# Block 0 of a token mixer's input: from one transposing DMA and a partly loaded strip to four plain loads and transposes on TensorE

## The chip, the cores and the metric

The kernel runs on one core of a Trainium2 chip. The metric is the device time of one execution in microseconds (us). Lower is better. The profile is of one execution on that core.

## The reference

All tensors are bfloat16. S = 2048 tokens, D = 512, 32 heads of 16. A branch (attention over 8 keys at distances 0, 2, ..., 14) and B branch (an MLP over the tokens) read the same x and are mixed by a gate.

```python
x = A_x                                                   # 2048 x 512
g = sigmoid((x * gate_w).sum(-1, keepdims=True))
q, k, v = split(x @ A_wqkv)                               # heads of 16
logits[s, w] = (q[s] . k[s - 2w]) * 16**-0.5              # w = 0..7, masked before the start
a = (softmax(logits) applied to v[s - 2w]) @ A_wo
h = layernorm(x)
u = gelu(einsum("sd,sf->df", h, B_w1) + B_b1)             # f = 1792, contraction over tokens
b = einsum("df,fs->sd", u, B_w2) + B_b2
return g * a + (1 - g) * b
```

## The kernel before

The kernel keeps everything in one arena of on-chip memory and names views of it. `X` holds x with tokens on the partitions (16 tiles of 128 tokens). `XT` holds x transposed, the 512 columns as four blocks `dt` of 128 partitions by 2048 tokens. `WQKV`, `W1W`, `W2S` and `WO` are the weights, `Q5`, `K5`, `V5` the projections, and `ps` is the accumulator memory of eight banks of 512 floats per partition.

The stages are these. TensorE first projects: for a token block `sb` of 512 and a quarter `dl` of the head dimensions, four matmuls (one for each `dt`) sum into one bank (`f_proj`, L613 to L621), and ScalarE (ACT) copies the bank to `Q5`, `K5` or `V5` (`f_evq`, L626 and L629). VectorE (DVE) multiplies Q by shifted K (L689), and TensorE sums the products over a head (L697). Between and after these TensorE does the MLP's two products (L811 and L861), and at the end the output product (L877), whose result DVE mixes with the gate (L898) before it is stored. DVE also takes the row statistics of the layer norm (L573, which reads `X`), the softmax and the sums over the values.

The order on each engine comes from a list scheduler (`_Sched`). Each operation is added by `A(engine, function, duration, reads, writes, ...)`, and the names in `reads` and `writes` give its waits. `chain([...])` (L958 on) fixes by hand the order on DVE and ACT. Loads are issued with `sch.dma(queue, ...)` on SP or ACT; on SP each load comes after the one before it (`prev_dma`) and waits for the one five back (`throttle`), through the list `init_dmas`. The attribute `lands` gives the scheduler a landing time of the first loads, and their waits are cleared.

Token block 0 is projected before the others, in an order that follows the landing of its parts: `pf_*`, L633 to L640. All eight banks are used, four for Q (`acc0` to `acc3`) and four for K (`lg4` to `lg7`). The four Q banks take `dt` 0, then 1, 2 and 3; then the four K banks take `dt` 0 and 1, then 2 and 3: 32 matmuls of 512 columns.

What block 0 needs comes in this way. ACT loads columns 0 to 127 of the first four x tiles into `XP` (L479), and then Wq's first 128 rows. SP issues a transposing DMA of columns 128 to 511 into `XT` blocks 1 to 3 (`ld_xt0`, L473), then Wq's other three parts, Wk in two loads, x tiles 0 and 1 (`ld_x`, for L573), the transposing DMA of block 1 (`ld_xt(1)`, L460), and x tiles 2 and 3. TensorE runs warm-up matmuls on constants (L536), transposes the four tiles of `XP` by a matmul with an identity (`f_tr`, L544), and runs two more warm-up matmuls. ACT (L554) and DVE (L556) copy the halves of the result to `XT` block 0. Only then, and when Wq's first part has landed, the projections begin.

Of the kernel before, what the change touches and what calls it, by code (L numbers as in the profile page):

```python
# [5 lines left out]
BF16 = mybir.dt.bfloat16  # L6
# [3 lines left out]
AF = mybir.ActivationFunctionType  # L10
# [323 lines left out]
def bass_gated_mix__sliding_local_dilated__mixer_token_mlp__prompt_kernel(nc, A_x, A_wqkv, A_wo, B_x, B_w1, B_b1, B_w2, B_b2, gate_w, out, dbg=None):  # L334
    with contextlib.ExitStack() as es:
        view, pview, off, total = _views(nc, es)
        ps = es.enter_context(nc.psum_tensor("ps", [128, 8, 512], FP32))
        esem = {e: es.enter_context(nc.semaphore("sem_" + e)) for e in ("pool", "act", "dve", "pe")}
        sch = _Sched()

        x2d = A_x[0]
        xv = x2d.rearrange("(t p) d -> p t d", p=128)
# [5 lines left out]
        X = view("X", BF16, [(D, NST), (1, D)])  # L348
        XT = view("XT", BF16, [(S, 4), (1, S)])
# [19 lines left out]
        IDENT = view("IDENT", BF16, [(1, 128)])  # L369
# [45 lines left out]
        A = sch.add  # L415
# [12 lines left out]
        def mk_dma(dst, src):  # L428
            return lambda e: e.dma_start(dst, src)  # L429

        init_dmas = []
# [4 lines left out]
        def prev_dma():  # L436
            return [init_dmas[-1]] if init_dmas else []

        def ld_x(t0, n, q="sp"):
            ds = sch.dsem("x%d" % t0)  # L440
            op = sch.dma(q, mk_dma(X[:, t0:t0 + n, :], xv[:, t0:t0 + n, :]), n * 128 * D * 2, ds,
                         writes=["x%d" % t for t in range(t0, t0 + n)], deps=throttle() if q == "sp" else [], after=prev_dma() if q == "sp" else [], name="d_x%d" % t0)
            if q == "sp":
                init_dmas.append(op)
            return op

        def ld_w(tn, d0, n, q="sp"):
            ds = sch.dsem("wqkv%d_%d" % (tn, d0))
            op = sch.dma(q, mk_dma(WQKV[:, d0:d0 + n, tn * D:(tn + 1) * D], wqkv_v[:, d0:d0 + n, tn * D:(tn + 1) * D]),
                         n * 128 * D * 2, ds, writes=["wqkv%d_%d" % (tn, dt) for dt in range(d0, d0 + n)],  # L450
                         deps=throttle() if q == "sp" and n == 4 else [], after=prev_dma() if q == "sp" else [],
                         issue=0.65 if n == 4 else 0.45, name="d_wp%d_%d" % (tn, d0))
            if q == "sp":
                init_dmas.append(op)
            return op
# [5 lines left out]
                         writes=["xt_%d" % t for t in range(4 * sb, 4 * sb + 4)], deps=throttle(), after=prev_dma(), name="d_xt%d" % sb)  # L461
            init_dmas.append(op)

        XT0 = ["xt0_%d" % d for d in range(4)] + ["xt0_0b"]
        ALLXT = XT0 + ["xt_%d" % t for t in range(4, NST)]

        def xt_of(sb, d0=0, d1=4):
            return XT0[d0:d1] + (XT0[4:] if d0 == 0 else []) if sb == 0 else ["xt_%d" % t for t in range(4 * sb, 4 * sb + 4)]

        def ld_xt0():  # L470
            ds = sch.dsem("xt0")
            dst = XT[:, 1:4, 0:512]
            op = sch.dma("sp", lambda e: e.dma_start_transpose(dst, x2d[0:512, 128:512]), 512 * 384 * 2, ds, issue=1.25,  # L473
                         writes=XT0[1:4], after=prev_dma(), name="d_xt0")
            init_dmas.append(op)
            return op

        XP = view("OUTS", BF16, [(128, 4), (1, 128)])
        d_xp = sch.dma("act", mk_dma(XP, xv[:, 0:4, 0:128]), 512 * 128 * 2, sch.dsem("xp"), writes=["outs0"], issue=0.4, name="d_xp")  # L479

        first_loads = [ld_w(0, 0, 1, "act"), ld_xt0(), ld_w(0, 1, 1), ld_w(0, 2, 1), ld_w(0, 3, 1), ld_w(1, 0, 2), ld_w(1, 2, 2),
                       ld_x(0, 2)]
        ld_xt(1)
        first_loads.append(init_dmas[-1])
        for op_, t_ in zip(first_loads, (3.4, 4.6, 5.0, 5.4, 5.8, 6.6, 7.4, 8.2, 10.6)):
            op_.lands = t_
            op_.deps.clear()
        d_xp.lands = 3.1
        first_loads[0].order.add(d_xp)
        init_dmas[:] = [first_loads[1]] + first_loads[5:]  # L490
        ld_x(2, 2)
        ld_x(4, 4)
        ld_xt(2)
        ld_xt(3)
# [5 lines left out]
        def ld_w1(j):  # L500
# [4 lines left out]
            if j < 4:  # L505
# [8 lines left out]
                       writes=["wo"], deps=throttle(), after=prev_dma(), name="d_wo")  # L514
# [4 lines left out]
        for i_, (v_, n_) in enumerate(((B_b1, NFT), (B_b2, NST))):  # L519
            vr = v_.rearrange("(t q j) -> q t j", q=4, j=32)  # L520
            for q_ in range(4):
                sch.dma("sp", mk_dma(psub(BR, 32 * q_, n_, 32 * i_, [(1, 32)]), vr[q_]), n_ * 64, ds_b, reads=["br"],
                        writes=["br_%d_%d" % (i_, q_)], deps=throttle(), after=prev_dma(), name="d_b_%d_%d" % (i_, q_), issue=0.45)
        d_w1.append(ld_w1(3))
        A("dve", lambda e: e.transpose(out=BT, in_=BR), 0.2, reads=["br_%d_%d" % (i_, q_) for i_ in range(2) for q_ in range(4)],
          writes=["btc"], name="t_b")
# [3 lines left out]
        CONE = nc.const_aps.tensor(1.0, [128, D], BF16)  # L530

        def f_warm(n, w_=D):
            def fn(e):
                ins = None
                for _ in range(n):
                    ins = e.matmul(ps[:, 7, 0:w_], lhsT=CONE[:, 0:128], rhs=CONE[:, 0:w_], start=True, stop=True)  # L536
                return ins
            return fn

        def f_tr(h):  # L540
            def fn(e):
                ins = None
                for t in range(2):
                    ins = e.matmul(ps[:, 5 + h, 128 * t:128 * t + 128], lhsT=XP[:, 2 * h + t, :], rhs=IDENT, start=True, stop=True)  # L544
                return ins
            return fn

        A("pe", f_warm(5), 2.13, writes=["lg7_0", "lg7_1"], name="warm1", prio=-100)
        w2_ = A("pe", f_warm(1, 256), 0.2, writes=["lg7_0", "lg7_1"], name="warm2", prio=-100)
        ta_ = A("pe", f_tr(0), 0.215, reads=["outs0", "ident"], writes=["lg5_0", "lg5_1"], after=[w2_], name="tr0", prio=-100)  # L550
        tr_ = A("pe", f_tr(1), 0.215, reads=["outs0", "ident"], writes=["lg6_0", "lg6_1"], after=[ta_], name="tr1", prio=-100)
        A("pe", f_warm(1), 0.43, writes=["lg7_0", "lg7_1"], after=[tr_], name="warm3", prio=-100)
        w3_ = A("pe", f_warm(1, 256), 0.2, writes=["lg7_0", "lg7_1"], after=[tr_], name="warm4", prio=-100)
        A("act", lambda e: e.activation(out=XT[:, 0, 0:256], in_=ps[:, 5, 0:256], func=AF.Copy), 0.35, reads=["lg5_0", "lg5_1"],  # L554
          writes=["xt0_0"], name="ev_tra", prio=0)
        A("dve", lambda e: e.tensor_copy(out=XT[:, 0, 256:512], in_=ps[:, 6, 0:256]), 0.35, reads=["lg6_0", "lg6_1"],  # L556
          writes=["xt0_0b"], name="ev_trb", prio=0)

        JK = view("OUTS", BF16, [(1, D)], extra=0)
        def cols(v_, lo, n, step=1):  # L560
# [9 lines left out]
        for hf in range(2):  # L570
            t0 = 8 * hf
            for t in range(t0, t0 + 8):
                A("dve", (lambda t_: (lambda e: e.bn_stats(out=ST6[:, t_, :], in_=X[:, t_, :])))(t), 0.59,  # L573
                  reads=["x%d" % t], writes=["st6_%d" % t], name="ln1_%d" % t, prio=0)
# [13 lines left out]
              reads=["zc%d" % hf], writes=["sd%d" % hf], name="ln_sqrt%d" % hf, prio=0)  # L588
            A("dve", (lambda t0_: (lambda e: e.reciprocal(out=cols(RSTD, t0_, 8), in_=cols(SD, t0_, 8))))(t0), 0.25,
              reads=["sd%d" % hf], writes=["rstd%d" % hf], name="ln_rstd%d" % hf, prio=0)  # L590
            A("dve", (lambda t0_: (lambda e: e.scalar_tensor_tensor(
                out=cols(NMR, t0_, 8), in0=mv(t0_, 0), scalar=-0.5, in1=cols(RSTD, t0_, 8),
# [38 lines left out]
        tnames = ["q", "k", "v"]  # L631
        first = [(tn, dl) for tn in range(2) for dl in range(4)]
        fbn = [["acc%d" % b] for b in range(4)] + [["lg%d_0" % b, "lg%d_1" % b] for b in range(4, 8)]  # L633
        for (b0, d0, d1, s0, s1) in ((0, 0, 1, 0, 512), (0, 1, 2, 0, 512), (0, 2, 3, 0, 512), (0, 3, 4, 0, 512), (4, 0, 2, 0, 512), (4, 2, 4, 0, 512)):
            for b in range(b0, b0 + 4):
                tn, dl = first[b]
                last_main[0] = A("pe", f_proj(tn, dl, 0, b, d0, d1, s0, s1), 0.216 * (d1 - d0) * (s1 - s0) / 512,
                                 reads=xt_of(0, d0, d1) + ["wqkv%d_%d" % (tn, dt) for dt in range(d0, d1)],
                                 writes=fbn[b], after=[last_main[0]], name="pf_%s%d_%d_%d" % (tnames[tn], dl, d0, s0))
                last_main[0].order.add(w3_)  # L640
        for b, (tn, dl) in enumerate(first):
            A("act", f_evq(tn, dl, 0, b), 0.52, reads=fbn[b] + (["k5pad"] if tn == 1 else []),
              writes=["%s5_%d_0" % (tnames[tn], dl)], name="ev_%s%d_0" % (tnames[tn], dl), prio=0)
# [7 lines left out]
        for (tn, dl, sb) in seq_proj:  # L651
# [18 lines left out]
                writes=["xa"] + ["wqkv%d_%d" % (tn, dt) for tn in range(3) for dt in range(4)], name="d_xa")  # L670
# [271 lines left out]
        def chain(names):  # L942
            for a_, b_ in zip(names, names[1:]):
                byname[b_].order.add(byname[a_])

        def ln1(*ts):
            return ["ln1_%d" % t for t in ts]

        def ln2(hf):
            return ["ln2%s%d" % (c_, hf) for c_ in "abcd"]  # L950
# [4 lines left out]
        def lnr(hf):  # L955
            return ["ln_rstd%d" % hf, "ln_nmr%d" % hf]

        chain(["rp", "ev_trb"] + ln1(0, 1, 2, 3) + ["qkm_0_0_0", "qkm_0_1_0"] + ln1(4, 5, 6, 7) + ln2(0)  # L958
              + ["qkm_0_2_0"] + lnr(0) + ["qkm_0_3_0", "qkm_0_0_2"] + ln1(8, 9) + ["qkm_0_1_2", "qkm_0_2_2", "qkm_0_3_2"] + ln1(*range(10, 16)) + ln2(1)
              + ["t_b", "qkm_1_0_0"] + lnr(1) + ["qkm_1_1_0"]  # L960
              + ["qkm_1_2_0", "qkm_1_3_0"] + gz(12, 13, 14, 15) + ["msk_0", "sm_ma0", "sm_mb0"] + gz(0, 1, 2) + [
# [90 lines left out]
```

## Time and profile before

| what | us |
|---|---|
| median of three runs | 168.57 (167.89 to 170.0) |
| the profiled execution | 168.47 |
| its span (first to last instruction) | 167.1 |
| TensorE (PE) busy | 163.1 |
| weight loads (PEld), beside PE | 77.7 |
| VectorE (DVE) busy | 151.3 |
| ScalarE (ACT) busy | 75.1 |

Times in the views count from the start of the span. A name with a small q (SPq, ACTq) is an engine's instruction queue; a DMA row on it tells when the transfer was issued and for how long that held the queue, not when it landed. Matmuls are pipelined: their start-to-start distance is their cost, and the mean duration of one is longer. Loads that plain DMAs bring show as `DMA_DIRECT2D`, transposing ones as `DMA_TRANSPOSE`. The granted clock was 1.00 throughout.

### The profile page before, as it was taken

To read this page: it belongs to the slowest core of one execution; us is meant where nothing else is said; L and a number is where in the kernel's file an instruction comes from. 1 tells how busy PE (TensorE), PEld (TensorE's weight loads), DVE (VectorE), ACT (ScalarE), POOL (GpSimd) and SP (SyncE) were. 2 spreads that over 40 slices of the span, in tenths; PEclk is the share of its full clock that TensorE was granted. 3 is DMA by queue.
4 is the path that set the end of the run, shared out by engine and by line. 5 is a ranking of instruction groups with operands and counts; after the bars stand their busy time and mean duration, and the time that the engine had idled before them with its cause. 6 is when DMAs were issued, how large, how long until landed. Compare 5 with 4: busy or idle time off the path is not lost.

```text
span 167.1 us, 2152 instructions
## 1 busy us (share of the span) xinstructions
PE 163.1 (98%) x860; PEld 77.7 (47%) x860; DVE 151.3 (91%) x154; ACT 75.1 (45%) x116; POOL 0.7 (0%) x8
## 2 busy tenths in 40 slices
PE   7799999999999999999999999999999999999994
PEld 3355555554554444444444444444444444444463
DVE  1037999999999999999999999999999999999896
ACT  3077788889899818792122221131231321310100
POOL 1000000000000000000000000000000000000000
PEclk9999999999999999999999999999999999999999
DMA  6999999959103847996789916463572570000454
GB/s 143 298 258 238 295 323 274 291 162 305 60 0 104 305 117 189 308 291 149 174 228 335 346 38 146 109 190 83 166 216 82 141 224 0 0 0 0 157 190 159
DMA packets 47625, 29.64 MB, mean 177 GB/s; under 512 B 9856, under 2 KB 46464, under 8 KB 47616
## 3 DMA queue, kind: packets, MB, share of 16 engines
q1 hardware_dynamic: 45120, 24.85, 54.3%
q10 hardware_dynamic: 2496, 4.66, 10.2%
q8 instruction: 7, 0.11, 0.3%
q14 instruction: 2, 0.02, 0.0%
HBM read 21.24 MB, written 2.10 MB: 140 GB/s over the span
## 4 chain that ended last, share of the span: by engine, by line
PE 93%; DMA 2%; DVE 2%; ACTq 0%; issue 0%
PE ps L811 29%; PE ps L861 29%; PE ps L618 25%; PE ps L877 6%; PE ps L697 4%; DMA arena<-in_A_wqkv_dram 2%; DVE arena L898 2%; ACTq L429 0%
## 5 line engine op out<-in xcount | busy, mean ns | idle before, releaser
L811 PE MATMUL ps<-arena 128*128 128x512 bf16 x224 | 48.7, 379 | 0.0
L861 PE MATMUL ps<-arena 128*128 128x512 bf16 x224 | 48.7, 379 | 0.0
L618 PE MATMUL ps<-arena 128*128 128x512 bf16 x192 | 41.8, 379 | 1.0 <-DMA arena<-in_A_wqkv_dram 1.0
L689 DVE TENSOR_TENSOR arena<-arena 128x4096 bf16<-128x4096 bf16 (+1 forms) x12 | 35.5, 2998 | 1.5 <-ACT arena L629 1.0
L796 DVE TENSOR_TENSOR arena<-arena 128x8192 bf16<-128x8192 bf16 x8 | 35.0, 4418 | 0.0
L811 PEld LDWEIGHTS ps<-arena 128*128 128x128 bf16 x224 | 21.9, 98 | 26.6 <-ACT arena L727 0.4
L861 PEld LDWEIGHTS ps<-arena 128*128 128x128 bf16 x224 | 21.9, 98 | 26.4
L618 PEld LDWEIGHTS ps<-arena 128*128 128x128 bf16 x192 | 21.6, 113 | 21.4 <-issue 1.7
L929 ACT ACTIVATE arena<-ps,arena 128x512 bf16<-128x512 f32 x16 | 12.5, 778 | 39.4 <-PE ps L861 39.4
L799 DVE TENSOR_TENSOR arena<-arena 128x4096 bf16<-128x4096 bf16 (+1 forms) x16 | 27.0, 1751 | 0.0
L629 ACT ACTIVATE arena<-ps 128x512 bf16<-128x512 f32 x32 | 18.5, 596 | 4.5 <-PE ps L618 4.5
L832 ACT ACTIVATE arena<-ps,arena 128x512 bf16<-128x512 f32 x14 | 9.6, 688 | 22.2 <-PE ps L811 16.7
L573 DVE BATCH_NORM_STATS2 arena<-arena 128x6 f32<-128x512 bf16 x16 | 10.0, 681 | 7.1 <-DMA arena<-in_A_x_dram 7.1
L877 PE MATMUL ps<-arena 128*128 128x512 bf16 (+1 forms) x80 | 14.2, 336 | 0.0
L898 DVE SCALAR_TENSOR_TENSOR arena<-ps,arena 128x512 bf16<-128x512 f32 (+1 forms) x20 | 11.5, 638 | 0.9 <-PE ps L877 0.7
L597 ACT ACTIVATE arena<-arena 128x512 bf16<-128x512 bf16 x16 | 12.2, 805 | 0.0
L626 ACT ACTIVATE arena<-ps 128x512 bf16<-128x512 f32 x16 | 9.0, 596 | 6.2 <-PE ps L618 6.1
L877 PEld LDWEIGHTS ps<-arena 128*128 128x128 bf16 x80 | 7.8, 98 | 6.2
L673 DVE SCALAR_TENSOR_TENSOR arena<-arena 128x512 bf16<-128x512 bf16 x16 | 10.1, 687 | 0.0
L743 DVE TENSOR_TENSOR arena<-arena 128x512 bf16<-128x512 bf16 (+4 forms) x11 | 7.3, 666 | 0.6 <-ACT arena L762 0.2
L697 PE MATMUL ps<-arena 128*32 128x512 bf16 x128 | 7.3, 380 | 0.0
L727 ACT ACTIVATE arena<-ps 128x512 bf16<-128x512 f32 x8 | 4.7, 592 | 4.6 <-PE ps L697 4.6
(42 smaller groups left out, 40.3 us busy)
## 6 DMA issues: line engine op xcount, KB each, us to landing
arena<-in_B_w_dram SPq DMA_DIRECT2D x7, 1024.0 KB, 8.5
arena<-in_B_w_dram SPq DMA_DIRECT2D x8, 896.0 KB, 5.1
arena<-arena ACTq DMA_DIRECT2D x32, 128.0 KB, 2.9
arena<-in_A_x_dram SPq DMA_DIRECT2D x4, 512.0 KB, 6.6
out_dram<-arena SPq DMA_DIRECT2D x14, 128.0 KB, 1.7
arena<-in_A_x_dram SPq DMA_DIRECT2D x1, 1536.0 KB, 8.0
arena<-in_A_wqkv_dram SPq DMA_DIRECT2D x2, 256.0 KB, 3.7
arena<-in_A_x_dram SPq DMA_DIRECT2D x2, 256.0 KB, 4.0
```

Source lines behind the costliest of these rows:

```text
L597: A("act", (lambda t_: (lambda e: e.activation(out=X[:, t_, :], in_=X[:, t_, :], func=AF.Identity, scale=col(RSTD, t_), bias=col(NMR, t_)) ...
L618: ins = e.matmul(ps[:, bank, s0:s1], lhsT=lhsT, rhs=XT[:, dt, sb * 512 + s0:sb * 512 + s1], start=(dt == 0 and s0 == 0), stop=(dt == 3))
L629: return lambda e: e.activation(out=dst, in_=ps[:, bank, :], func=AF.Copy)
L689: return lambda e: e.tensor_tensor(out=PBL[buf][:, :, 512 * c0:512 * (c0 + nc_)], in0=in0, in1=in1, op=ALU.mult)
L697: ins = e.matmul(ps[32 * c:32 * c + 32, 4 + wl, :], lhsT=RP, rhs=PBL[buf][:, wl, c * 512:(c + 1) * 512], start=(dl == 0), stop=(dl == 3), ...
L796: A("dve", (lambda o_, i0, i1: (lambda e: e.tensor_tensor(out=o_, in0=i0, in1=i1, op=ALU.mult)))(pv, in0, in1), 4.4, reads=v_res + ["atx_% ...
L799: A("dve", (lambda pv_, n__: (lambda e: e.tensor_tensor(out=pv_[:, 0:n__], in0=pv_[:, 0:n__], in1=pv_[:, n__:2 * n__], op=ALU.add)))(pv, n ...
L811: ins = e.matmul(ps[:, bank, :], lhsT=W1W[:, slot, st, 128 * e_:128 * e_ + 128], rhs=X[:, st, :], start=(st == 0), stop=(st == NST - 1))
L861: ins = e.matmul(ps[:, bank, :], lhsT=W2S[slot][:, ft, 128 * e_:128 * e_ + 128], rhs=UT[:, ft, :], start=(ft == 0), stop=(ft == NFT - 1))
L877: ins = e.matmul(ps[:, bank, 0:c1 - c0], lhsT=OT[:, t, 128 * i:128 * i + 128], rhs=WO[:, t, c0:c1], start=(t == 0), stop=(t == 3))
L898: A("dve", (lambda i_, b_, c0_, c1_: (lambda e: e.scalar_tensor_tensor(out=T1[:, i_, c0_:c1_], in0=ps[:, b_, 0:c1_ - c0_], scalar=col(G, i ...
L929: A("act", (lambda i_, bank_: (lambda e: e.activation(out=T1[:, i_, :], in_=ps[:, bank_, :], func=AF.Identity, scale=col(OMG, i_), bias=co ...
```

## The change

Block 0 of x is loaded whole, as four plain loads of one tile (128 tokens by 512 columns, 128 KB) each, straight into `X`: tiles 0 and 2 on SP, tiles 1 and 3 on ACT. TensorE transposes them in two groups of eight 128 x 128 blocks, tiles 0 and 1 first (`tr0a`, `tr0b`), then tiles 2 and 3 (`tr1a`, `tr1b`), after five warm-up matmuls on constants that now write bank 3. Of each group ACT copies the columns of `dt` 0 and 1 to `XT` and DVE those of `dt` 2 and 3. The transposing DMA in front, the load into `XP`, the two later warm-up matmuls and the later loads of x tiles 0 to 3 are gone. Wq's four parts and Wk's two all come on SP, behind tiles 0 and 2. The first projections of `dt` 0 and 1 are cut in two: 256 tokens of group 0 first, then the 256 of group 1. The instructions of each engine after this first part keep their order.

```diff
-        first_loads = [ld_w(0, 0, 1, "act"), ld_xt0(), ld_w(0, 1, 1), ld_w(0, 2, 1), ld_w(0, 3, 1), ld_w(1, 0, 2), ld_w(1, 2, 2),
-                       ld_x(0, 2)]
+        first_loads = [ld_x(0, 1), ld_x(2, 1), ld_x(1, 1, "act"), ld_x(3, 1, "act"), ld_w(0, 0, 1), ld_w(0, 1, 1), ld_w(0, 2, 1), ld_w(0, 3, 1),
+                       ld_w(1, 0, 2), ld_w(1, 2, 2)]
         ld_xt(1)
         first_loads.append(init_dmas[-1])
...
-        d_xp.lands = 3.1
-        first_loads[0].order.add(d_xp)
-        init_dmas[:] = [first_loads[1]] + first_loads[5:]
-        ld_x(2, 2)
+        first_loads[3].order.add(first_loads[2])
+        init_dmas[:] = first_loads[6:]
         ld_x(4, 4)
...
-        def f_tr(h):
+        def f_tr(p_, h):
             def fn(e):
                 ins = None
-                for t in range(2):
-                    ins = e.matmul(ps[:, 5 + h, 128 * t:128 * t + 128], lhsT=XP[:, 2 * h + t, :], rhs=IDENT, start=True, stop=True)
+                for dt in range(2 * h, 2 * h + 2):
+                    for t in range(2 * p_, 2 * p_ + 2):
+                        c0 = 256 * (dt % 2) + 128 * (t % 2)
+                        ins = e.matmul(ps[:, 4 + 2 * p_ + h, c0:c0 + 128], lhsT=X[:, t, 128 * dt:128 * dt + 128], rhs=IDENT,
+                                       start=True, stop=True)
                 return ins
             return fn
...
-        A("pe", f_warm(5), 2.13, writes=["lg7_0", "lg7_1"], name="warm1", prio=-100)
-        w2_ = A("pe", f_warm(1, 256), 0.2, writes=["lg7_0", "lg7_1"], name="warm2", prio=-100)
-        ta_ = A("pe", f_tr(0), 0.215, reads=["outs0", "ident"], writes=["lg5_0", "lg5_1"], after=[w2_], name="tr0", prio=-100)
-        tr_ = A("pe", f_tr(1), 0.215, reads=["outs0", "ident"], writes=["lg6_0", "lg6_1"], after=[ta_], name="tr1", prio=-100)
-        A("pe", f_warm(1), 0.43, writes=["lg7_0", "lg7_1"], after=[tr_], name="warm3", prio=-100)
-        w3_ = A("pe", f_warm(1, 256), 0.2, writes=["lg7_0", "lg7_1"], after=[tr_], name="warm4", prio=-100)
...
+        pw_ = A("pe", f_warm(4), 1.71, writes=["acc3"], name="warm1", prio=-100)
+        pw_ = A("pe", f_warm(1, 256), 0.2, writes=["acc3"], after=[pw_], name="warm2", prio=-100)
+        for p_ in range(2):
+            for h in range(2):
+                bn = 4 + 2 * p_ + h
+                lgr = ["lg%d_0" % bn, "lg%d_1" % bn]
+                pw_ = A("pe", f_tr(p_, h), 0.43, reads=["x%d" % (2 * p_), "x%d" % (2 * p_ + 1), "ident"], writes=lgr, after=[pw_],
+                        name="tr%d%s" % (p_, "ab"[h]), prio=-100)
+                dst = XT[:, 2 * h:2 * h + 2, 256 * p_:256 * p_ + 256]
+                pin = ps[:, bn, :].rearrange("p (d c) -> p d c", d=2)
+                if h == 0:
+                    A("act", ...activation(out=dst, in_=pin, func=AF.Copy), writes=["xt0_%da" % p_], name="ev_tra%d" % p_)
+                else:
+                    A("dve", ...tensor_copy(out=dst, in_=pin), writes=["xt0_%db" % p_], name="ev_trb%d" % p_)
...
-        for (b0, d0, d1, s0, s1) in ((0, 0, 1, 0, 512), (0, 1, 2, 0, 512), (0, 2, 3, 0, 512), (0, 3, 4, 0, 512), (4, 0, 2, 0, 512), (4, 2, 4, 0, 512)):
+        for (b0, d0, d1, s0, s1) in ((0, 0, 1, 0, 256), (0, 1, 2, 0, 256), (0, 0, 1, 256, 512), (0, 1, 2, 256, 512),
+                                     (0, 2, 3, 0, 512), (0, 3, 4, 0, 512), (4, 0, 2, 0, 512), (4, 2, 4, 0, 512)):
...
-        chain(["rp", "ev_trb"] + ln1(0, 1, 2, 3) + ...
+        chain(["rp"] + ["ev_trb0", "ev_trb1"] + ln1(0, 1, 2, 3) + ...
```

The two `A(...)` calls of the copies are shortened here.

More of the change, by code (lines that the diff above doesn't have):

```diff
@@ L462, in ld_xt, with xt_of @@
             init_dmas.append(op)
-        XT0 = ["xt0_%d" % d for d in range(4)] + ["xt0_0b"]
+        XT0 = ["xt0_%d%s" % (p_, h) for p_ in range(2) for h in "ab"]
         ALLXT = XT0 + ["xt_%d" % t for t in range(4, NST)]
[L467 to L479, printed above, removed]
-        first_loads = [ld_w(0, 0, 1, "act"), ld_xt0(), ld_w(0, 1, 1), ld_w(0, 2, 1), ld_w(0, 3, 1), ld_w(1, 0, 2), ld_w(1, 2, 2),
-                       ld_x(0, 2)]
+        def xt_of(sb, d0=0, d1=4, s0=0, s1=512):
+            if sb:
+                return ["xt_%d" % t for t in range(4 * sb, 4 * sb + 4)]
+            return ["xt0_%d%s" % (p_, h) for p_ in range(s0 // 256, s1 // 256) for h in "ab"[d0 // 2:(d1 + 1) // 2]]
+        first_loads = [ld_x(0, 1), ld_x(2, 1), ld_x(1, 1, "act"), ld_x(3, 1, "act"), ld_w(0, 0, 1), ld_w(0, 1, 1), ld_w(0, 2, 1), ld_w(0, 3, 1),
+                       ld_w(1, 0, 2), ld_w(1, 2, 2)]
         ld_xt(1)
         first_loads.append(init_dmas[-1])
-        for op_, t_ in zip(first_loads, (3.4, 4.6, 5.0, 5.4, 5.8, 6.6, 7.4, 8.2, 10.6)):
+        for op_, t_ in zip(first_loads, (2.9, 3.8, 2.9, 3.8, 4.3, 4.7, 5.1, 5.5, 6.4, 7.3, 10.0)):
             op_.lands = t_
             op_.deps.clear()
-        d_xp.lands = 3.1
-        first_loads[0].order.add(d_xp)
-        init_dmas[:] = [first_loads[1]] + first_loads[5:]
-        ld_x(2, 2)
+        first_loads[3].order.add(first_loads[2])
+        init_dmas[:] = first_loads[6:]
         ld_x(4, 4)
@@ L535, in fn @@
                 for _ in range(n):
-                    ins = e.matmul(ps[:, 7, 0:w_], lhsT=CONE[:, 0:128], rhs=CONE[:, 0:w_], start=True, stop=True)
+                    ins = e.matmul(ps[:, 3, 0:w_], lhsT=CONE[:, 0:128], rhs=CONE[:, 0:w_], start=True, stop=True)
                 return ins
             return fn
-        def f_tr(h):
+        def f_tr(p_, h):
             def fn(e):
                 ins = None
-                for t in range(2):
-                    ins = e.matmul(ps[:, 5 + h, 128 * t:128 * t + 128], lhsT=XP[:, 2 * h + t, :], rhs=IDENT, start=True, stop=True)
-                return ins
-            return fn
@@ L553, in bass_gated_mix__sliding_local_dilated__mixer_token_mlp__prompt_kernel @@
-        w3_ = A("pe", f_warm(1, 256), 0.2, writes=["lg7_0", "lg7_1"], after=[tr_], name="warm4", prio=-100)
[L554 to L557, printed above, removed]
+                for dt in range(2 * h, 2 * h + 2):
[3 more added lines that the diff above has]
+                                       start=True, stop=True)
@@ new lines, in fn @@
+                return ins
+            return fn
+        pw_ = A("pe", f_warm(4), 1.71, writes=["acc3"], name="warm1", prio=-100)
[9 more added lines that the diff above has]
+                if h == 0:
+                    A("act", (lambda d_, i_: (lambda e: e.activation(out=d_, in_=i_, func=AF.Copy)))(dst, pin), 0.6,
+                      reads=lgr, writes=["xt0_%da" % p_], name="ev_tra%d" % p_, prio=0)
+                else:
+                    A("dve", (lambda d_, i_: (lambda e: e.tensor_copy(out=d_, in_=i_)))(dst, pin), 0.72,
+                      reads=lgr, writes=["xt0_%db" % p_], name="ev_trb%d" % p_, prio=0)
@@ L559, in bass_gated_mix__sliding_local_dilated__mixer_token_mlp__prompt_kernel @@
+        w3_ = pw_
         JK = view("OUTS", BF16, [(1, D)], extra=0)
@@ L637, in bass_gated_mix__sliding_local_dilated__mixer_token_mlp__prompt_kernel @@
                 last_main[0] = A("pe", f_proj(tn, dl, 0, b, d0, d1, s0, s1), 0.216 * (d1 - d0) * (s1 - s0) / 512,
-                                 reads=xt_of(0, d0, d1) + ["wqkv%d_%d" % (tn, dt) for dt in range(d0, d1)],
+                                 reads=xt_of(0, d0, d1, s0, s1) + ["wqkv%d_%d" % (tn, dt) for dt in range(d0, d1)],
                                  writes=fbn[b], after=[last_main[0]], name="pf_%s%d_%d_%d" % (tnames[tn], dl, d0, s0))
@@ L956, in lnr @@
             return ["ln_rstd%d" % hf, "ln_nmr%d" % hf]
-        chain(["rp", "ev_trb"] + ln1(0, 1, 2, 3) + ["qkm_0_0_0", "qkm_0_1_0"] + ln1(4, 5, 6, 7) + ln2(0)
+        chain(["rp"] + ["ev_trb0", "ev_trb1"] + ln1(0, 1, 2, 3) + ["qkm_0_0_0", "qkm_0_1_0"] + ln1(4, 5, 6, 7) + ln2(0)
               + ["qkm_0_2_0"] + lnr(0) + ["qkm_0_3_0", "qkm_0_0_2"] + ln1(8, 9) + ["qkm_0_1_2", "qkm_0_2_2", "qkm_0_3_2"] + ln1(*range(10, 16)) + ln2(1)
```

## The prediction

> **What bounds the kernel now.** I read first the busy shares and then the chain that ended last, to see which engine the end follows.
>
> ```profile
> PE 163.1 (98%) x860; PEld 77.7 (47%) x860; DVE 151.3 (91%) x154; ACT 75.1 (45%) x116; POOL 0.7 (0%) x8
> ```
>
> ```profile
> 0.80 0.45 ACTq L429
> 1.25 0.03 issue
> 1.28 4.08 DMA arena<-in_A_wqkv_dram
> 5.36 0.09 issue
> 5.45 32.97 PE ps L618 x152
> 38.41 3.57 PE ps L697 x64
> ...
> 161.50 3.98 DVE arena L898 x9
> ```
>
> The second fence is the chain in order of time (start, length, what). From 5.45 us to 161.50 it lies on TensorE without a break, through the projections (L618), the logit sums (L697), both MLP products (L811, L861) and the output product (L877). Ahead of it stands one transfer: Wq's first 128 rows, issued by ACT at 1.28, landed at 5.36. So the end follows the start of the first projection. Then the timeline of the first 14 us (start, length, engine, line, operation; in brackets the idle time before):
>
> ```profile
> 0.80 1.35 SPq L473 DMA_TRANSPOSE arena<-in_A_x_dram  x1
> 0.84 2.50 PE L536 MATMUL ps<-const-bfloat16-1.0 128*128 128x512 bf16 x6 [0.84 <-PEq L1037]
> 3.16 0.61 PE L544 MATMUL ps<-arena 128*128 128x128 bf16 x4
> 3.57 0.84 PE L536 MATMUL ps<-const-bfloat16-1.0 128*128 128x512 bf16 x2
> 3.60 0.38 ACT L554 ACTIVATE arena<-ps 128x256 bf16<-128x256 f32 x1 [0.47 <-PE ps L544]
> 3.81 0.43 DVE L556 CAST arena<-ps 128x256 bf16<-128x256 f32 x1 [2.31 <-PE ps L544]
> 5.26 3.67 SPq L460 DMA_TRANSPOSE arena<-in_A_x_dram  x1
> 5.45 8.79 PE L618 MATMUL ps<-arena 128*128 128x512 bf16 x40 [1.04 <-DMA arena<-in_A_wqkv_dram]
> 9.17 1.29 DVE L573 BATCH_NORM_STATS2 arena<-arena 128x6 f32<-128x512 bf16 x2 [4.94 <-DMA arena<-in_A_x_dram]
> 14.91 4.49 DVE L689 TENSOR_TENSOR arena<-arena 128x4096 bf16<-128x4096 bf16 x2 [1.04 <-ACT arena L629]
> ```
>
> Three things are to be seen. The column part of block 0 that TensorE transposes is in the arena by 4.24; PE then idles 1.04 us for Wq. DVE is idle for 4.94 us before L573, so early DVE work is free. DVE's dense part begins at 14.91 on an evacuation by ACT of TensorE's own work, so it moves with TensorE. Last, the speed of TensorE: the warm-up of 5.5 times 512 columns takes from 0.84 to 3.16, 0.42 us for 512; from 5.45 on, 40 matmuls take 8.6 us, 0.216 for 512. The rate doubled somewhere between 4.41 and 5.45, though the granted clock stands at 1.00 in every window.
>
> How fast loads come, from the DMA issues (KB each, us to landing) and two windows of the first microseconds (the last column is GB/s):
>
> ```profile
> arena<-in_A_x_dram ACTq DMA_DIRECT2D x1, 128.0 KB, 2.2
> arena<-in_A_wqkv_dram ACTq DMA_DIRECT2D x1, 128.0 KB, 4.1
> ```
>
> ```profile
> 5.50:6.00 0.50, 0.50 (x3) 0.29 (x4) 0.00 (x0) 0.00 (x0) 0.00 (x0) 1.00 1.07 338
> 6.00:6.50 0.50, 0.50 (x4) 0.23 (x2) 0.00 (x0) 0.00 (x0) 0.00 (x0) 1.00 1.12 361
> ```
>
> Two loads issued 0.5 us apart on ACT took 2.2 and 4.1 us. The second shared the 16 engines with the front transposing DMA (L473), whose packets are small; plain loads alone ran at 338 to 361 GB/s, 128 KB (131 KB in thousands) in 0.37 us.
>
> **Part by part.** *Removed:* the transposing DMA of 384 KB in front (1.35 us of SP's issue, 4.8 us to landing), the partial load of x (128 KB), Wq's first load on ACT, four transposes with their two copies (L554, L556), three of the eight warm-up matmuls (two of 512 columns, one of 256), and later the two loads x0-1 and x2-3 (512 KB together). *Added:* four plain loads of 128 KB (x0, x2 on SP; x1, x3 on ACT), 16 transposes of 128 columns, two evacuations of 512 columns on ACT and two on DVE, and the first eight matmuls of 512 columns become 16 of 256.
>
> Loads. x0 and x1 are issued at 0.80, as the 2.2 us row was. Together they hold 256 KB, against its 128: 3.02 if larger pieces make up for it, 3.39 with 0.37 more. I take 3.1. x2 and x3 are issued at about 1.28 and lie behind them: 0.74 more at 350 GB/s, 3.85. The bounds are 3.5 (no gap) and 5.36 (the 4.1 us row, issued at the same 1.28). I take 3.85, since the small-piece stream that the 4.1 us row shared engines with is gone. Wq's four parts follow on SP, issued at about 1.75, 2.2, 2.65 and 3.1 (0.45 each, the issue time of the same form now): landing 4.2, 4.6, 5.0 and 5.3 at 0.37 each. Wk's two 256 KB follow at 6.1 and 6.8.
>
> TensorE. Warm-up: four times 0.425 and one of 0.21 from 0.84, done issuing at 2.75. It idles until x0 and x1. Transposes: L544 took 0.41 for four, 0.103 each. Eight from 3.15 end at 3.97; x2 and x3 are there by then, so the other eight end at 4.8. Wq's first part landed at 4.2, so the first projection starts at 4.85 instead of 5.45: **-0.60 us**. If x2 and x3 land at 3.5, x0 and x1 at 3.0, the start is 4.7; at 5.36, it is 5.4 + 0.82 = 6.2.
>
> Evacuations. A transposed pair of 512 columns on ACT costs 0.6 (L626, 596 ns, same form but for one more dimension), on DVE between 0.43 (L556, half as wide) and 0.86; I take 0.72. The first ACT copy runs 3.8 to 4.4, ahead of the start. The second half's begins when four transposes of that group are done, near 4.6, and ends at 5.2; it is first needed after eight matmuls of 256 columns, 4.85 + 0.87 = 5.7. DVE's second copy ends near 5.8 and is needed at 4.85 + 1.75 = 6.6. Each costs nothing while it has that half microsecond or more; if the cover went, TensorE would wait for the difference. Behind them on DVE stands L573, with 4.9 us of idle time before it; on ACT the first projection evacuation, which began at 8.45.
>
> Smaller matmuls. 256 columns cost 0.109 in the tail (the 32 of that form in L877 keep PE busy for 3.7 us, some 0.2 of it the last one's end), against 0.108 for half of 512. A weight load of L618 takes 113 ns, so 16 could take 1.81 against 1.72. Between +0.02 and +0.09; I take **+0.06**.
>
> Clock. The first full-rate matmul that the trace shows starts at 5.45, after 3.57 us of unbroken half-rate work (0.84 to 4.41). With a start at 4.85, the first 0 to 0.6 us of projections may run at half rate and lose half of that, 0 to 0.3. I take **+0.15**. That the pause from 2.75 to 3.1 makes it later is a rival below.
>
> What follows. xt1 is issued at about 4.45 instead of 5.26, with 1536 KB ahead of it instead of 1792: it landed at 5.26 + 5.9 = 11.2, and comes some 0.8 earlier, 10.4. It is needed after the first 32 matmuls, 4.85 + 7.1 = 11.9: no wait. The later loads of x, Wv and W1 each move up with it. x0 to x3 are there from the start, so L573's first four run in DVE's idle time and not from 9.17 on; DVE's dense part still waits for ACT's copies and moves with TensorE. All later work keeps its order, and the chain shows no wait on a load after 5.45, so the shift reaches the end whole.
>
> Sum: -0.60 + 0.06 + 0.15 = **-0.39 us**. The profiled execution took 168.47 (span 167.1, 1.37 around it), so 168.1. The median of the three runs, 168.57, lies 0.1 above that execution, well inside their spread of 167.89 to 170.0; I keep **168.1**.
>
> **The rivals.**
>
> *The clock stays low (slower).* Place: the first projections. The 3.57 us of unbroken work at half rate are now cut by the pause at 2.75, and the rest of it is transposes. If the account restarts at 3.1, the full rate comes at 3.1 + 3.57 = 6.7, or, by the distance from 0.84 to 5.45, as late as 7.7; the projections run at half rate from 4.85 until then and lose half, 0.9 to 1.4. If only projections and warm-up count, it restarts at 4.85: 8.4 to 9.5, a loss of 1.8 to 2.3. In place of 0.15 this gives 168.8 to 170.2, 169.3 in the middle. It is slower than before once the full rate comes later than about 5.95 (0.54 gained, twice that lost time). For it: the trace shows no full-rate matmul before 3.6 us of work. Against: four transposes stood inside that work and a pause of 1.04 behind it, and the rate was full at 5.45. [...]
>
> *The loads come late (slower).* If four loads on two queues and Wq slow each other as the 4.1 us row was slowed, x2 and x3 land at 5.36, the start is 6.2, the sum +0.75 + 0.06: 169.3. It decides from a landing at 4.55 (5.45 less 0.86 of transposes). For it, that row; against it, the 338 to 361 GB/s as soon as plain loads run alone.
>
> *No gain.* Wq's first part, now fifth on the queues, lands no earlier than 5.36 (its issue moves from 1.28 to 1.75): 168.5. Against: 640 KB at 350 GB/s is 1.9 us after the first bytes.
>
> *More gain.* Loads at their lower bounds, and the second eight transposes at twice the rate (0.41): 3.05 + 0.82 + 0.41 and a semaphore's way put the start near 4.4 to 4.5, no clock loss, some 0.9 gained: 167.6. Against: the weight loads of L544, 131 ns each, do not shrink with the columns.
>
> **How the numbers follow.** Forecast 0.43, low clock 0.24, late loads 0.14, no gain 0.10, more gain 0.09. The forecast's own range is 167.6 to 168.6. To hold 8 in 10 it reaches up through most of the two slow cases and down past the larger gain with the runs' spread: 167.1 to 169.8. A change of over 2% (3.4 us; about what a measurement of this kernel can tell from no change) would mean under 165.2 or over 171.9. No case reaches the first; the second needs a late load and a low clock together. So faster 0.01, same 0.95, slower 0.04.
>
> **What would show it.** First projection at 4.7 to 5.0, after 16 transposes with at most a short pause between the eights, the wait ahead of the transposes on x and none on Wq; matmuls of 256 columns at 0.11 apart from the first or by the fourth; no PE pause afterwards; L697 first at 38.0 instead of 38.4. Wrong, if the first projection comes after 5.45, if 256 columns stay at 0.21 for more than a microsecond, or if a PE pause shows behind the first 32.

## The result, and the profile after

| | before | after |
|---|---|---|
| median of 22 runs each | 168.39 us (167.58 to 170.65) | 169.4 us (167.89 to 170.46) |
| the profiled execution, its span | 168.47, 167.1 | 169.06, 167.8 |

The changed kernel is slower by 0.59% (ratio 1.0059, 95% interval 1.0037 to 1.008). The ratio leaves out executions more than 1.5% above the fastest of their kernel, three of the kernel before (170.19 to 170.65) and one of the changed one (170.46); over all 22 each the means are 168.63 and 169.40, 0.46% apart.

The chain that ended last, in order of time (start, length, what), shows where it begins and that it keeps its distance to the end:

```profile
0.80 2.75 DMA arena<-in_A_x_dram
3.54 0.14 issue
3.68 1.87 PE ps L535 x16
5.54 5.07 PE ps L617 x28
...
39.10 3.57 PE ps L697 x64
...
162.19 3.98 DVE arena L898 x9
```

L697 begins 0.69 us later than before (39.10 against 38.41), and so does the last piece (162.19 against 161.50). Whatever was lost was lost before L697, and after it nothing was lost or won. The timeline of the start:

```profile
0.84 2.08 PE L525 MATMUL ps<-const-bfloat16-1.0 128*128 128x512 bf16 x5 [0.84 <-PEq L1037]
3.68 1.87 PE L535 MATMUL ps<-arena 128*128 128x128 bf16 x16 [0.76 <-DMA arena<-in_A_x_dram]
4.73 0.69 DVE L554 CAST arena<-ps 128x512 bf16<-128x512 f32 x1 [3.23 <-PE ps L535]
5.16 0.60 ACT L551 ACTIVATE arena<-ps 128x512 bf16<-128x512 f32 x1 [0.26 <-PE ps L535]
5.34 10.89 PE L617 MATMUL ps<-arena 128*128 128x256 bf16 x53
6.19 2.46 DVE L572 BATCH_NORM_STATS2 arena<-arena 128x6 f32<-128x512 bf16 x4
```

The first projection starts at 5.34, only 0.11 earlier than before. TensorE pauses for 0.76 us ahead of the transposes (2.92 to 3.68), waiting for x, and not between the two groups. Then the projections themselves, L617 in two stretches, from 5.3 to 6.6 and from 7.1 to 7.8 (durations in ns: least, median, most):

```profile
L617 PE MATMUL ps<-arena x6: 421/421/422, 5.3 to 6.4; 128*128 128x256 bf16 x6
...
L617 PE MATMUL ps<-arena x9: 272/273/317, 6.8 to 7.7; 128*128 128x256 bf16 x9
```

The same instruction of 256 columns lasts 421 ns in the first stretch and 273 in the second; the starts lie 0.213 and 0.109 apart, and the change comes at 6.9. The 16 of them take 5.34 to 7.86, 2.52 us, where 16 at 0.109 would take 1.75. So 0.77 lost to half rate, 0.02 to the smaller matmuls, 0.11 won by the start: +0.68, the 0.69 that the chain shows.

The loads, from the DMA issues (KB each, median us to landing):

```profile
arena<-in_A_wqkv_dram SPq DMA_DIRECT2D x4, 128.0 KB, 3.2
arena<-in_A_x_dram ACTq DMA_DIRECT2D x2, 128.0 KB, 2.8
arena<-in_A_x_dram SPq DMA_DIRECT2D x2, 128.0 KB, 2.6
```

In the trace x0 and x1 landed at 3.37 and 3.54, x2 and x3 at 3.94 and 4.18, Wq's first part at 4.98. So in this execution the start hung on x0 and x1: the 16 transposes began at 3.68 and ran 0.107 apart until 5.34, and Wq was there before they ended.

### The profile page after: what moved, and what is told of

The parts are those of the page before. It is cut to its first block, busy times and chain, and to the rows that moved or that the text cites. A ratio compares the mean times of both kernels' runs of the same rounds, so it can differ in the third digit from the quotient of the medians.

```text
span 167.8 us, 2175 instructions
## 1 busy us (share of the span) xinstructions
PE 163.1 (97%) x863; PEld 79.7 (48%) x877; DVE 152.0 (91%) x155; ACT 75.8 (45%) x117; POOL 0.7 (0%) x8
## 4 chain that ended last, share of the span: by engine, by line
PE 94%; DVE 2%; DMA 2%; issue 1%
PE ps L861 29%; PE ps L811 29%; PE ps L617 25%; PE ps L877 6%; PE ps L697 4%; DVE arena L898 2%; DMA arena<-in_A_x_dram 2%; PE ps L535 1%
## 5 line engine op out<-in xcount | busy, mean ns | idle before, releaser
L861 PE MATMUL ps<-arena 128*128 128x512 bf16 x220 | 48.5, 379 | 0.2
L811 PE MATMUL ps<-arena 128*128 128x512 bf16 x219 | 48.2, 379 | 0.4 <-issue 0.2
L617 PE MATMUL ps<-arena 128*128 128x512 bf16 (+1 forms) x196 | 42.2, 376 | 0.3 <-ACT arena L585 0.2
L811 PEld LDWEIGHTS ps<-arena 128*128 128x128 bf16 x224 | 21.8, 98 | 26.6 <-ACT arena L727 0.4
L861 PEld LDWEIGHTS ps<-arena 128*128 128x128 bf16 x224 | 21.9, 98 | 26.5
L617 PEld LDWEIGHTS ps<-arena 128*128 128x128 bf16 x200 | 22.8, 115 | 19.3 <-ACT arena L596 0.4
L877 PE MATMUL ps<-arena 128*128 128x512 bf16 (+1 forms) x79 | 14.1, 336 | 0.1
L877 PEld LDWEIGHTS ps<-arena 128*128 128x128 bf16 x80 | 7.8, 98 | 6.2
L572 DVE BATCH_NORM_STATS2 arena<-arena 128x6 f32<-128x512 bf16 x16 | 9.9, 679 | 0.0
L697 PE MATMUL ps<-arena 128*32 128x512 bf16 x128 | 7.3, 380 | 0.0
```

Of the source, the lines that this page charges most:

```text
L617: ins = e.matmul(ps[:, bank, s0:s1], lhsT=lhsT, rhs=XT[:, dt, sb * 512 + s0:sb * 512 + s1], start=(dt == 0 and s0 == 0), stop=(dt == 3))
L697: ins = e.matmul(ps[32 * c:32 * c + 32, 4 + wl, :], lhsT=RP, rhs=PBL[buf][:, wl, c * 512:(c + 1) * 512], start=(dl == 0), stop=(dl == 3), ...
L811: ins = e.matmul(ps[:, bank, :], lhsT=W1W[:, slot, st, 128 * e_:128 * e_ + 128], rhs=X[:, st, :], start=(st == 0), stop=(st == NST - 1))
L861: ins = e.matmul(ps[:, bank, :], lhsT=W2S[slot][:, ft, 128 * e_:128 * e_ + 128], rhs=UT[:, ft, :], start=(ft == 0), stop=(ft == NFT - 1))
L877: ins = e.matmul(ps[:, bank, 0:c1 - c0], lhsT=OT[:, t, 128 * i:128 * i + 128], rhs=WO[:, t, c0:c1], start=(t == 0), stop=(t == 3))
```

## The experiments

Three theories of the half rate were tested. Theory A was that the rate of TensorE doubles only after some 3.6 us of unbroken work, so that the new pause costs it. Theory B was that transposes do not count as work for it. Theory C was that the late loads are all, and the ramp does not hang on this work.

**E1: the pause filled** (and once more as E11). Two more warm-up matmuls of 512 columns in the changed kernel.

```diff
-        pw_ = A("pe", f_warm(4), 1.71, writes=["acc3"], name="warm1", prio=-100)
+        pw_ = A("pe", f_warm(6), 2.56, writes=["acc3"], name="warm1", prio=-100)
```

> The changed kernel with two more warm-up matmuls of 512 columns, so that TensorE is busy from 0.84 us until x lands near 3.5 and the pause of 0.76 us ahead of the transposes goes. Theory A (the rate doubles after some 3.6 us of unbroken work, and the pause restarts that account): full rate between 4.4 and 5.4, all 256-column projections 0.11 apart, first projection at 5.0 to 5.3, L697 first at 38.0 to 38.3, span 166.7 to 167.1, time 0 to 0.4 us below before. Theory B (transposes do not count, warm-up and projections do, a pause only suspends): 2.8 us counted by 3.6, 0.8 of projections at half rate, full rate near 6.1, span near 167.4. Theory C (the ramp does not hang on this work; the loss is the landing of x): as the changed kernel, full rate near 6.9, span near 167.8.

Median 168.62; the changed kernel on the same chip (E4) 169.25; ratio to before 1.0028 (0.9992 to 1.0064). TensorE in its timeline:

```profile
3.61 1.42 PE L535 MATMUL ps<-arena 128*128 128x128 bf16 x16
5.77 3.45 PE L617 MATMUL ps<-arena 128*128 128x256 bf16 x23 [0.74 <-DMA arena<-in_A_wqkv_dram]
```

The step of the transposes falls from 0.107 to 0.056 at 3.9, among the transposes, 3.0 us after the first matmul and sooner than the 4.4 to 5.4 of A, and every projection runs 0.109 apart. B and C each expected half-rate projections here; both are out as the whole story. What is left ahead of the projections is a wait of 0.74 on Wq's first part, which landed at 5.72 in this execution. The start that A expected, 5.0 to 5.3, was missed by that, and with it the span (167.5, not 166.7 to 167.1).

**E2: the kernel before without its later warm-up.** `warm3` and `warm4` are left out, so TensorE idles from 3.6 to the first projection.

```diff
-        A("pe", f_warm(1), 0.43, writes=["lg7_0", "lg7_1"], after=[tr_], name="warm3", prio=-100)
-        w3_ = A("pe", f_warm(1, 256), 0.2, writes=["lg7_0", "lg7_1"], after=[tr_], name="warm4", prio=-100)
+        w3_ = tr_
```

> The kernel before without the two warm-up matmuls behind the transposes, so that unbroken work ends at 3.6 us (2.7 us of it) and TensorE idles 1.9 us until the first projection. Theory A: the account restarts at 5.45, full rate near 8.7 to 9.0, 1.6 to 1.8 us lost, span 168.7 to 168.9. Theory B: 2.3 us counted by 3.2, 1.3 of projections at half rate, 0.6 lost, span near 167.7. Theory C: no change, span 167.1.

Executions from 167.67 to 170.27, median 169.72, ratio 1.0061 (1.0002 to 1.012). In the profiled one (span 169.0) Wq landed at 4.49 and the first projection started at 4.58. The projections of 512 columns in two stretches (durations in ns):

```profile
L617 PE MATMUL ps<-arena x13: 588/631/631, 4.6 to 9.7; 128*128 128x512 bf16 x13
...
L617 PE MATMUL ps<-arena x7: 379/379/441, 10.1 to 11.4; 128*128 128x512 bf16 x7
```

They ran at half rate, a step of 0.427, until 10.2. That is later than A expected, 8.7 to 9.0, and the span lies where A put it only because the start was earlier: some 13 matmuls lost 0.211 each, 2.7 us, and the start gained 0.87, which leaves the 1.9 that the span grew. Two of the six executions, at 167.67 and 168.66, show no such loss. A fixed amount of work after a restart does not fit; the moment differs between executions.

**E3: a short warm-up** in the changed kernel.

```diff
-        pw_ = A("pe", f_warm(4), 1.71, writes=["acc3"], name="warm1", prio=-100)
+        pw_ = A("pe", f_warm(1), 0.43, writes=["acc3"], name="warm1", prio=-100)
```

> The changed kernel with a warm-up of one matmul of 512 and one of 256 columns, so that TensorE is busy from 0.84 to 1.48 and then idles until x lands. Theory A: the pause restarts the account anyway, so nothing changes: full rate near 6.9, span near 167.8. Theory B: 0.6 us counted ahead of the transposes in place of 2.1, so full rate 1.4 us later, near 8.3, 0.7 us lost, span near 168.5. Theory C: no change.

Median 169.64, ratio 1.0085 (1.0046 to 1.0123); in the profiled execution the full rate came at 8.1, with Wq's first part landed at 5.69. This is near the 8.3 that B expected and not A's 6.9, so B had to be tried directly (E5).

**E4: the changed kernel again**, with no edit.

> The changed kernel unaltered, for a second profile of it on the chip of the others. If the full rate comes again within 0.2 us of 6.9, it is set by the kernel's own work; if it moves by a microsecond between executions, something that runs free of the kernel has a part in it, and theories A and B each hold only on the mean.

Median 169.25. Full rate at 6.5 in this profile, against 6.9, with x 0.08 us later and Wq's first part at 5.45: neither within 0.2 nor off by a microsecond. It left the question open.

**E5: three times the transposes.** E3's kernel with each transpose issued three times.

```diff
-                for dt in range(2 * h, 2 * h + 2):
+                for dt in 3 * list(range(2 * h, 2 * h + 2)):
```

> The kernel of the short warm-up with every transpose issued three times (48 in place of 16, the same result), so that some 5 us of transposes stand ahead of the first projection and little else. [...]

The matmuls of L535 from 3 to 6.7 us and from 6.95 to 8, and then those of L617 (durations in ns: least, median, most; first and last start):

```profile
L535 PE MATMUL ps<-arena x28: 257/311/311, 3.8 to 6.6; 128*128 128x128 bf16 x28
...
L535 PE MATMUL ps<-arena x20: 219/219/219, 6.7 to 7.8; 128*128 128x128 bf16 x20
...
L617 PE MATMUL ps<-arena x15: 272/273/273, 7.9 to 9.4; 128*128 128x256 bf16 x15
```

The step of the transposes fell from 0.107 to 0.056 at 6.7, 2.9 us after the first of them, with 0.64 us of other work long before it. By B nothing but those 0.64 us would have been work, so B is out; this rests on one execution (170.8 us).

**E6: the pause of the kernel before filled** (and once more as E12). Two more warm-up matmuls behind `warm4`.

```diff
+        w3_ = A("pe", f_warm(2), 0.86, writes=["lg7_0", "lg7_1"], after=[w3_], name="warm5", prio=-100)
```

> The kernel before with two more warm-up matmuls of 512 columns ahead of the first projection, into its pause of 1.04 us. [...]

Twelve executions from 167.7 to 169.18, median 168.62. Of the 29 of the kernel before beside it, seven lay at 170.0 to 170.7 and none between 168.72 and 170.0. The upper group was gone with the pause. The ratio, which still holds two of the seven (170.0 and 170.14), is 0.9998 (0.9967 to 1.003); beside the other 22 alone, whose mean is 168.20, the filled kernel with a mean of 168.51 is 0.31 slower. So the kernel before seems to have the changed kernel's loss too, in some executions, and then a larger one. No execution of its upper group was profiled; the nearest is E2's, at 170.27.

**E7, E8, E9, E10: other orders of the loads**, all on E1's filled kernel, to get Wq's first part sooner. E7 issues it second on SP, ahead of x2. E8 issues Wq's first two parts ahead of x2, and projects the first half of block 0 between the two groups of transposes. E9 loads x in two loads of 256 KB on SP with Wq's first part alone on ACT, and projects both halves of `dt` 0 ahead of `dt` 1. E10 has Wq's second part on ACT too.

```diff
 E7    first_loads = [ld_x(0, 1), ld_w(0, 0, 1), ld_x(2, 1), ld_x(1, 1, "act"), ld_x(3, 1, "act"), ld_w(0, 1, 1), ...
 E8    first_loads = [ld_x(0, 1), ld_w(0, 0, 1), ld_w(0, 1, 1), ld_x(2, 1), ld_x(1, 1, "act"), ld_x(3, 1, "act"), ...
 E9    first_loads = [ld_x(0, 2), ld_x(2, 2), ld_w(0, 0, 1, "act"), ld_w(0, 1, 1), ...
 E10   first_loads = [ld_x(0, 2), ld_x(2, 2), ld_w(0, 0, 1, "act"), ld_w(0, 1, 1, "act"), ...
...
 E8    if (s0, s1) == (0, 256): last_main[0].order.add(trs[1]); trs[2].order.add(last_main[0])
 E9, E10   for (b0, d0, d1, s0, s1) in ((0, 0, 1, 0, 256), (0, 0, 1, 256, 512), (0, 1, 2, 0, 256), (0, 1, 2, 256, 512), ...
```

> The filled changed kernel with Wq's first load issued second on SP, ahead of x2. In the filled kernel the clock was full from 3.9 and the first projection waited until 5.77 for Wq's first part, which landed at 5.72. If that landing is what held it: Wq's first part at 4.0 to 4.6, x2 and x3 at 4.2 to 4.6, first projection at 4.7 to 5.2, span 166.5 to 166.9, 0.2 to 0.6 us below before. If it is transposes, copies or the clock: start and span as in the filled kernel, 5.7 and 167.4.

> As the last one, with Wq's first two parts ahead of x2 on SP, and TensorE projecting the first half of block 0 (dt 0 and 1) between the two groups of transposes. If loads and the clock were all that stood against the change: first projection near 4.5, 0.45 us of transposes behind it, span 166.3 to 166.8, 0.3 to 0.8 us below before. If the clock comes late in some executions they lie up to 1 us higher.

> The filled changed kernel with x tiles 0 to 3 in two loads of 256 KB, both on SP, Wq's first part alone on ACT, issued at 0.8, the other parts behind x on SP, and both halves of dt 0 projected ahead of dt 1. In all the runs so far the third load on SP, issued near 1.7, landed at 5.0 to 5.7 whatever it held, one or two of its 16 shares late by up to 1 us. If that goes with the place in the queue: Wq's first part at 3.0 to 3.6, x at 3.4 and 4.3, Wq's second (third on SP) at 5.0 to 5.7, needed at 5.7; first projection at 4.8 to 5.0, span 166.5 to 166.9, 0.2 to 0.6 us below before. If it goes with the bytes ahead (640 KB landed by 5.2 to 5.7 in any order): the last of x or of Wq's first part lands past 4.8, first projection past 5.4, no gain.

> As the last one with Wq's second part on ACT too, behind the first. By place in the queue: both on ACT by 4.2, x at 3.4 and 4.3, Wq's third part (third on SP) at 5.0 to 5.7 and needed at 6.6, so nothing waits: first projection 4.8 to 5.0, span 166.5 to 166.9. By bytes ahead: x's second load shares the engines with both parts of Wq and lands near 5, first projection 5.5 or later, span 167.2 or more.

| | median | ratio to before (95%) | landed in the profiled execution | first projection |
|---|---|---|---|---|
| E7 | 168.77 | 1.0021 (0.9995 to 1.0047) | Wq's first 3.97, x2 5.23 | 6.11 |
| E8 | 169.17 | 1.0049 (1.0025 to 1.0073) | Wq's first 3.96, second 5.64, x2 5.99 | 5.05 |
| E9 | 168.74 | 1.0022 (0.9999 to 1.0046) | Wq's first 3.69, x 4.20 and 4.92 | 5.99 |
| E10 | 168.98 | 1.0048 (1.0029 to 1.0067) | Wq's 3.62 and 4.57, x 4.19 and 5.31 | 5.82 |

All four missed what the gain needed. E7 also had one execution at 171.21, of which there is no profile; its other eleven lie at 168.12 to 169.12. Whichever load is put forward lands early, and another takes its place: the first 640 KB were down at 5.23 in E7, 5.64 in E8 and 4.92 in E9, against 4.98 to 5.72 in the changed kernel and E1, E3, E4. E9 and E10 speak for the bytes ahead and not for the place in the queue. Bytes were not all that held these starts. E8 also waited for copies, 0.35 and 0.47 us on ACT ahead of its two groups of projections, and its first four projections ran at half rate. E9's start was set by x's first load and the transposes behind it. TensorE in the timeline of E9 shows the clock again:

```profile
4.33 1.87 PE L534 MATMUL ps<-arena 128*128 128x128 bf16 x16 [0.56 <-DMA arena<-in_A_x_dram]
5.99 3.28 PE L616 MATMUL ps<-arena 128*128 128x256 bf16 x22
```

x's first load, twice the size, landed at 4.20, the warm-up had ended issuing at 3.57, and with the pause between, the 16 transposes ran at half rate to the end. In E10 a pause as long was followed by the full rate at 4.6, behind the third transpose:

```profile
4.32 0.72 PE L535 MATMUL ps<-arena 128*128 128x128 bf16 x8 [0.55 <-DMA arena<-in_A_x_dram]
```

So a pause does not restart an account, which takes theory A in its strict form out too.

**E11 and E12: both kernels filled, on one chip.**

> The filled changed kernel once more, beside the filled kernel before on one chip, to see what the loads and transposes alone are worth once TensorE has no pause in front in either. If the 640 KB that stand ahead of the first projection in both set the start: both the same within 0.3%, medians 168.3 to 168.7, and no execution at 170 or more in either. If the change's loads are the better ones once the clock is equal: 0.3 to 0.5 us below the filled kernel before.

> The filled kernel before, beside the last one: median 168.3 to 168.7, nothing above 169.3, while the kernel before itself again shows about one execution in five at 170.0 to 170.7 and none between 169.3 and 169.9.

Medians 168.52 (168.13 to 168.88) and 168.57 (168.28 to 168.87), 12 runs each; ratios to before 1.0014 (0.9999 to 1.0029) and 1.0007 (0.9984 to 1.0029). The kernel before beside them had a median of 168.34, three of 23 executions at 170.6 to 170.75, and one at 169.87, where none was expected. The chain of E11 around the first projection (start, length, what):

```profile
1.72 3.64 DMA arena<-in_A_wqkv_dram
5.36 0.05 issue
5.41 33.02 PE ps L617 x160
```

And the chain of E12 there:

```profile
5.01 0.38 issue
5.38 32.97 PE ps L619 x152
```

With the clock equal, the first projection starts at 5.41 and 5.38, and the two filled kernels cannot be told apart. Filling the pause is worth 0.63 us on the changed kernel on one chip (169.25 of E4 against 168.62 of E1), and 0.73 against E11 on another. On the kernel before it takes the upper group away; its mean moves from 168.74 to 168.51 beside E6 and from 168.63 to 168.57 beside E12, its median not down. No version beat the kernel before in the median. Against the 19 executions of the kernel before beside E12 that lie below 169.3 (mean 168.24), the filled ones are slower, with means of 168.50 (E11) and 168.57. Why is open, and so a rival to "the two sets of loads are worth the same" stands untested: the added matmuls of E6 and E12 run until about 5.0 to 5.1 and may hold back a start whose Wq is there sooner, as at 4.49 in E2. No profile here shows such an execution.

## Why the prediction was wrong

It forecast 168.1, 0.39 us below the profiled execution; measured were +0.59 there and +0.99 by the ratio. The range held the time; the direction was wrong. The rival that came nearest is the low clock, put at 168.8 to 170.2, but its time is in part luck: it took the start at 4.85 and a loss of 0.9 to 1.4, and measured were 5.34 and 0.77, two errors that offset each other. Its account that restarts at the pause is not what E10 shows.

- **Loads: the step that failed first.** x0 and x1 were put at 3.1 and landed at 3.54; x2 and x3 at 3.85, landed 4.18; Wq's first part at 4.2, landed 4.98 to 5.72. The start was to move by -0.60 and moved by -0.11. Each load was taken to land behind the one before it, at the steady rate of 338 to 361 GB/s. The mean rate, some 300, was not far below that, as three windows of the changed kernel show (the last column is GB/s):

```profile
2.00:3.00 1.00, 0.92 (x3) 0.15 (x1) 0.00 (x0) 1.00 (x1) 0.00 (x0) 1.00 1.01 313
3.00:4.00 1.00, 0.32 (x4) 0.35 (x5) 0.00 (x0) 0.01 (x1) 0.00 (x0) 1.00 0.97 291
4.00:5.00 1.00, 1.00 (x12) 1.00 (x10) 0.27 (x1) 0.60 (x1) 0.00 (x0) 1.00 1.01 299
```

From 2 to 5 us they add up to 0.90 MB, and the five loads hold 0.66 MB (640 KB), so the loads issued behind them had a part of it. The trace counts a load's landing in 16 shares: of Wq's second and third parts the first shares were down at 4.48 and 4.92, ahead of the last share of the first part at 4.98. In E1, 14 of the 16 shares of Wq's first load were there by 4.82, and the last two came at 5.18 and 5.72. Up to 6.5 us nine packets of 1 KB took 0.5 to 1.3 us in the changed kernel's trace and eight took 0.4 to 1.2 in E1's, where the usual one took 0.046; in the kernel before there was one, of 0.74. Why these were slow stays open.
- **The premise under it.** The prediction treated the front transposing DMA as what held Wq up before. The bytes point elsewhere: before, 128 KB of x, 128 KB of Wq and 384 KB of the transposing DMA stood in front, 640 KB, and landed by 5.55 (Wq at 5.36); after, 512 KB of x and 128 KB of Wq, 640 KB again. What changed is that the first projection now needs all of them and the transposes behind them. The case "no gain", for which Wq's first part had to land no earlier than 5.36, came close on the start: 5.34, 5.50, 5.74, 5.77 and 5.41 in the five profiles with the changed kernel's loads and its 16 transposes.
- **Clock: the term that was mis-sized most.** Taken at +0.15, measured +0.77. The prediction named the pause as a rival and held against it that the kernel before was at full rate behind a pause of 1.04. That was one profiled execution, and E6 and E12 speak for the pause costing the kernel before too, in about one of five: with that pause filled, no execution in 24 lay above 169.2, without it 10 of the 52 beside them lay at 170.0 or more.
- **Right:** the smaller matmuls (+0.02 to +0.09 said, +0.02 found), the copies (0.60 on ACT, 0.72 said and 0.69 found on DVE) with the cover that was named for them, L572 in DVE's idle time, xt1 (10.4 said, 10.70 landed, first needed near 13.0), no pause of TensorE behind the first 32 matmuls' work, and that the shift of the start reaches the end whole.

What sets the moment of the full rate was not shown. With the first matmul at 0.84 (0.83 in E7), it came between 3.9 and 10.2. The two right columns are estimates, worked out from the starts that the traces show, with 0.427 us for 512 columns at half rate (fewer in proportion) as work. Idle time is the rest, so a pause counts from the end of the last step and comes out some 0.2 us longer than in the timelines:

| run | full rate at, us | half-rate work before it, us | idle since the first matmul, us |
|---|---|---|---|
| E1 | 3.9 | 3.0 | 0.0 |
| E10 | 4.6 | 3.0 | 0.8 |
| E11 | 4.9 | 4.0 | 0.1 |
| E8 | 5.8 | 4.3 | 0.7 |
| E9 | 6.2 | 4.6 | 0.8 |
| E7 | 6.2 | 4.5 | 0.9 |
| E4 | 6.5 | 4.6 | 1.1 |
| E5 | 6.7 | 3.5 | 2.3 |
| changed kernel | 6.9 | 5.1 | 1.0 |
| E3 | 8.1 | 4.7 | 2.6 |
| E2 | 10.2 | 8.4 | 1.0 |

It came early where TensorE had hardly been idle (E1, E11) and mostly later where it had paused, but no amount of work fits all these runs, with 3.0 us in E1 and 8.4 in E2, and no amount of idle time, with 2.3 us in E5 and 1.0 in E2, whose full rate came 3.5 us later. E9 and E10 had the same work and the same pause up to 4.3, and their full rate came at 6.2 and 4.6. That something which runs free of the kernel has a part in it is the author's estimate from such differences between executions; it was not measured.

## What to carry to other kernels

Where the first real work of TensorE waits for a load, keep it busy with warm-up matmuls right up to the landing: 0.76 us of pause went with 0.77 lost to half-rate matmuls in the profiled execution, filling it won 0.63 in the median (E1 beside E4), and the loss differed between executions (E2: 167.67 to 170.27), so look at the spread of the times and not at one profile. A filler of fixed length may have a price of its own: the filled kernels lay some 0.3 us above the usual executions of the kernel before (168.50 and 168.57 against 168.24). Count the bytes that must land before the first useful instruction; reordering and splitting the same bytes over two queues moved the wait from one load to another here (E7 to E10, first projection at 5.05 to 6.11), and the last of a load's 16 shares set it, not the mean rate (E1: 14 shares by 4.82, the last at 5.72, the first projection at 5.77). When the step that a profile shows as a wait is removed, ask what the start then needs instead.

## What was not expected of the hardware

- The granted clock reads 1.00 in all windows, those from 1.5 to 3 us of the changed kernel among them, while the step of 512 columns is 0.427 us in its warm-up and 0.215 from 7.9 us on; the rate at the start must be read from the distance of matmuls, not from that column.
- The rate doubled among transposes, written here as plain matmuls with an identity (E5, at 6.7 us), and at full rate their step fell from 0.107 to 0.056 us, below the 0.098 us that each of their weight loads lasted there. The prediction held the weight loads (0.131 each before) against a faster step; at full rate they did not prevent it.
- In the first microseconds single packets of 1 KB took up to 1.3 us, where the usual one took 0.046, and a load of 128 KB took 3.3 us (changed kernel) and 4.0 us (E1) to land when some 512 KB had been issued within a microsecond ahead of it.
